# A chunk-selected attention with a mixture of experts: every expert on every token, against every expert on its own tokens

## The chip, the cores and the metric

One core of a Trainium2 chip runs the whole kernel. The time is that of one launch on the device, in microseconds (us). The engines are PE (TensorE: matmuls and transposes), ACT (ScalarE), DVE (VectorE), POOL (GpSimd) and SP (SyncE, which here only issues DMAs). A queue written SPq or PEq is the sequencer of that engine.

## The reference, cut to what matters

```python
# attention: B=4 batches, H=8 heads, S=768 positions, D=64
ub = np.sum(np.maximum(q[:, :, :, None, :] * k_min[:, :, None, :, :], q[:, :, :, None, :] * k_max[:, :, None, :, :]), axis=-1)
...
top_chunks = np.argsort(ub, axis=-1)[..., -top_k:]      # 6 of 24 chunks of 32 keys
scores = np.where(mask, scale * (q @ k.T), -1e9)         # mask: chosen chunks, causal
attn = softmax(scores); attn_out = attn @ v
x = attn_out.transpose(0, 2, 1, 3).reshape(3072, 512)

# experts: N=3072 tokens, D=512, E=8, F=512
y_dense = np.maximum(x @ w1_dense, 0.0) @ w2_dense
logits = x @ w_gate; expert_idx = np.argmax(logits, axis=1); gate_w = softmax(logits)[expert_idx]
for e in range(E):
    mask = expert_idx == e
    h = np.maximum(x[mask] @ w1[e], 0.0)
    y_moe[mask] = gate_w[mask, None] * (h @ w2[e])
out = y_dense + y_moe
```

Each token has one expert; the dense layer takes every token.

## The kernel before, in words

Tile, the framework that the kernel is written in, places the semaphores, rotates the buffers of each pool and orders the instructions of each engine by a priority that follows the order of the program, so that neighbouring steps are interleaved.

**Attention** runs over 16 pairs of heads (`p`; four to a batch). SP loads q, k and v of a pair (`load`, six DMAs of 192 KB with rows of 64 floats) two pairs ahead; POOL casts them to half precision (`cast`); PE transposes k and q (`prep_k`, `prep_q`); PE and DVE find the sixth-best chunk bound (`prep_ub`); PE transposes q with the chosen-chunk mask beside it (`prep_s`). `scores` then makes the scores of both heads for one of six pieces (PE), their exponentials (ACT, 128x1024 at a time, line 191) and the causal corners (POOL, line 195). `av` multiplies by v (line 215), and `norm` writes the result to `xbig`, which stays in SBUF. The preparation of pair p+1 is put between the pieces of pair p.

**Weights.** After attention, SP loads every weight as float32 through three staging buffers (72 pieces of 256 KB) and DVE casts each to half precision (`load_cast`, lines 276 to 278). The staging pool is closed before the pools of the next stage open on the same bytes.

**Experts.** Six groups of 512 tokens follow. For each group, 16 transposes and copies make `xT` (lines 305 and 306), the gate gives `gvec`, a weight for each token and expert that is zero except at the token's own expert (lines 312 to 327), and `layer` is called nine times: for the dense weights and for each of the eight experts, on all 512 tokens. A layer is 16 matmuls for the hidden part (line 336), four relus (line 340), 16 matmuls for the output (line 344), four copies scaled by `gvec` (line 352) and four additions to `acc` (line 353). SP stores the four `acc` tiles at the end of a group.

Of the kernel before, what the change touches and what calls it, by code (L numbers as in the profile page):

```python
# [17 lines left out]
def kernel(  # L18
# [12 lines left out]
    nc = tc.nc  # L31
# [9 lines left out]
    const = ctx.enter_context(tc.tile_pool(name="const", bufs=1))  # L41
    HP = H // 2
    NP = B * HP

# [4 lines left out]
    exf = const.tile([128, S], HF)  # L49
    nc.gpsimd.memset(exf[0:32], -30000.0)  # L50
    nc.gpsimd.affine_select(out=exf[0:32], in_=exf[0:32], compare_op=ALU.is_ge, fill=0.0,
                            base=0, pattern=[[1, S]], channel_multiplier=-32)
    nc.gpsimd.affine_select(out=exf[0:32], in_=exf[0:32], compare_op=ALU.is_ge, fill=0.0,
# [14 lines left out]
    xbig = const.tile([128, NM, Dm], HF)  # L68

    NB = 2  # L70
    kT = [[const.tile([128, S], HF, name=f"kT{i}_{g}") for g in range(2)] for i in range(NB)]
    q16 = [const.tile([128, NT, 256], HF, name=f"q16_{i}") for i in range(NB)]
    v16 = [const.tile([128, 2, NT, D + 1], HF, name=f"v16_{i}") for i in range(3)]
    for i in range(NB):
        nc.vector.memset(kT[i][0], 0.0)
        nc.vector.memset(kT[i][1], 0.0)
        nc.vector.tensor_copy(kT[i][0][0:32, :], exf[0:32])
        nc.vector.tensor_copy(kT[i][1][64:96, :], exf[0:32])
        nc.gpsimd.memset(q16[i], 0.0)
    for i in range(3):  # L80
        nc.gpsimd.memset(v16[i][:, :, :, D : D + 1], 1.0)

# [7 lines left out]
        [(5, 640, 768)],  # L90
    ]
    last_of = {}
    for pi, pc in enumerate(PIECES):
        for bb, a, z in pc:
            for t in range(a // 128, z // 128):
                last_of[t] = (pi, bb)

    with (
        tc.tile_pool(name="aload", bufs=3) as aload,
        tc.tile_pool(name="ahead", bufs=2) as ahead,  # L100
        tc.tile_pool(name="aexp", bufs=3) as aexp,
        tc.tile_pool(name="psc", bufs=2, space=bass.MemoryType.PSUM) as psc,
        tc.tile_pool(name="pout", bufs=1, space=bass.MemoryType.PSUM) as pout,
        tc.tile_pool(name="pprep", bufs=2, space=bass.MemoryType.PSUM) as pprep,
    ):
# [10 lines left out]
        def cast(p):  # L116
            s = st[p]
            s["k16"] = k16 = ahead.tile([128, NT, 2, D], HF, name="k16")
            nc.gpsimd.tensor_copy(k16, s["k"].rearrange("p g t d -> p t g d"))
            nc.gpsimd.tensor_copy(q16[p % NB][:, :, 64:192].rearrange("p t (g d) -> p t g d", g=2),  # L120
                                  s["q"].rearrange("p g t d -> p t g d"))
            nc.gpsimd.tensor_copy(v16[p % 3][:, :, :, 0:D], s["v"])
# [26 lines left out]
        def prep_ub(p):  # L149
# [13 lines left out]
            sc = q16[p % NB][:, 1:NT, :]  # L163
            sc = bass.AP(sc.tensor, sc.offset, [sc.ap[0], sc.ap[1], [192, 2], [1, NC]]) if False else None
# [4 lines left out]
        def prep_s(p):  # L169
            s = st[p]  # L170
            s["r"] = []
            for g in range(2):
                ps = pprep.tile([128, S], HF, name="pp")
                for t in range(NT):
                    nc.tensor.transpose(ps[:, t * 128 : (t + 1) * 128], q16[p % NB][:, t, g * 128 : (g + 1) * 128], ident)  # L175
                r = ahead.tile([128, S], HF, name=f"r{g}")
                nc.vector.tensor_copy(r, ps)  # L177
                s["r"].append(r)

        def scores(p, i):  # L180
            s = st[p]
            sp = psc.tile([128, 2, 512], FP, name="sp")
            wid = sum(z - a for _, a, z in PIECES[i])
            for g in range(2):
                o = 0
                for bb, a, z in PIECES[i]:
                    nc.tensor.matmul(sp[:, g, o : o + z - a], kT[p % NB][g][:, bb * 128 : (bb + 1) * 128],  # L187
                                     s["r"][g][:, a:z], start=(o == 0), stop=True, skip_group_check=True)
                    o += z - a
            ex = aexp.tile([128, 2, 512], HF, name="ex")  # L190
            nc.scalar.activation(ex[:, :, :wid], sp[:, :, :wid], AF.Exp, scale=0.125)  # L191
            o = 0
            for bb, a, z in PIECES[i]:
                if a == bb * 128:
                    nc.gpsimd.affine_select(out=ex[:, :, o : o + 128], in_=ex[:, :, o : o + 128], compare_op=ALU.is_ge,  # L195
                                            fill=0.0, base=0, pattern=[[0, 2], [1, 128]], channel_multiplier=-1)
                o += z - a
            s["ex", i] = ex

        def av(p, i):  # L200
            s = st[p]
            if i == 0:
                s["op"] = pout.tile([128, 2, 512], FP, name="op")
            op = s["op"]
            ex = s["ex", i]
            for g in range(2):
                o = 0
                seq = []
                for bb, a, z in PIECES[i]:
                    for t in range(a // 128, z // 128):  # L210
                        seq.append((t == bb, bb, t, o + t * 128 - a))
                    o += z - a
                seq.sort(key=lambda e: e[0])
                for n, (_, bb, t, c) in enumerate(seq):
                    nc.tensor.matmul(op[:, g, t * (D + 1) : (t + 1) * (D + 1)], ex[:, g, c : c + 128],  # L215
                                     v16[p % 3][:, g, bb, :], start=(i == 0 and n == 0),
                                     stop=(last_of[t] == (i, bb)), skip_group_check=True)
# [9 lines left out]

        load(0)
        load(1)
        cast(0)  # L230
        prep_k(0)
        prep_q(0)
        prep_ub(0)
        prep_s(0)
        for p in range(NP):
            if p + 2 < NP:
                load(p + 2)
            nx = p + 1 if p + 1 < NP else None
            if nx is not None:
                cast(nx)  # L240
            scores(p, 0)
            scores(p, 1)
            if nx is not None:
                prep_k(nx)
                prep_q(nx)
            av(p, 0)
            scores(p, 2)
            av(p, 1)
            if nx is not None:
                prep_ub(nx)  # L250
            scores(p, 3)
            av(p, 2)
            scores(p, 4)
            av(p, 3)
            if nx is not None:
                prep_s(nx)
            scores(p, 5)
            av(p, 4)
            av(p, 5)
            norm(p)  # L260

    WD = HF
    wpool = ctx.enter_context(tc.tile_pool(name="wpool", bufs=1))
    w1d = wpool.tile([128, NK, F], WD)
    w2d = wpool.tile([128, NK, Dm], WD)
    w1e = wpool.tile([128, NK, E, F], WD)
    w2e = wpool.tile([128, NK, E, Dm], WD)
    wg = wpool.tile([128, NK, E], WD)

    with tc.tile_pool(name="stg", bufs=3) as stg:  # L270
        wgs = stg.tile([128, NK, E], FP)
        nc.sync.dma_start(out=wgs, in_=moe_w_gate.rearrange("(ko ki) e -> ki ko e", ki=128))
        nc.vector.tensor_copy(wg, wgs)

        def load_cast(dst, src_ap):
            s2 = stg.tile(list(dst.shape), FP, tag="lc")
            nc.sync.dma_start(out=s2, in_=src_ap)
            nc.vector.tensor_copy(dst, s2)  # L278

        for ko in range(NK):  # L280
            load_cast(w1d[:, ko], moe_w1_dense[ko * 128 : (ko + 1) * 128, :])
            load_cast(w2d[:, ko], moe_w2_dense[ko * 128 : (ko + 1) * 128, :])
            for e in range(E):
                load_cast(w1e[:, ko, e], moe_w1[e, ko * 128 : (ko + 1) * 128, :])
                load_cast(w2e[:, ko, e], moe_w2[e, ko * 128 : (ko + 1) * 128, :])

    MB = 4
    with (
        tc.tile_pool(name="mx", bufs=2) as mx,
        tc.tile_pool(name="mh", bufs=3) as mh,  # L290
        tc.tile_pool(name="mts", bufs=3) as mts,
        tc.tile_pool(name="macc", bufs=2) as macc,
        tc.tile_pool(name="mg", bufs=2) as mg,
        tc.tile_pool(name="mpt", bufs=2, space=bass.MemoryType.PSUM) as mpt,
        tc.tile_pool(name="mph", bufs=2, space=bass.MemoryType.PSUM) as mph,
        tc.tile_pool(name="mpy", bufs=3, space=bass.MemoryType.PSUM) as mpy,
        tc.tile_pool(name="mpg", bufs=1, space=bass.MemoryType.PSUM) as mpg,
    ):
        for mb in range(NM // MB):
            xT = mx.tile([128, NK, MB * 128], WD)  # L300
            for mi in range(MB):
                xm = xbig[:, mb * MB + mi, :]
                for ko in range(NK):
                    tp = mpt.tile([128, 128], WD)
                    nc.tensor.transpose(tp, xm[:, ko * 128 : (ko + 1) * 128], ident)  # L305
                    nc.scalar.mul(xT[:, ko, mi * 128 : (mi + 1) * 128], tp, 1.0)  # L306

            gl = mpg.tile([128, MB, E], FP)
            gvec = mg.tile([128, MB, E], FP)
            for mi in range(MB):  # L310
# [80 lines left out]
```

## Time and profile before

| | |
|---|---|
| median of 2 runs | 662.7 us (662.58 to 662.82) |
| the profiled execution | 664.45 us, its span 662.7 us |
| mean granted TensorE clock | 0.914 of full speed |
| busy share of the span | PE 78%, ACT 59%, DVE 45%, POOL 13% |
| packets of under 512 B | 77328 of 89660 |
| HBM read, written | 37.77 MB, 6.29 MB |

The span runs from the first to the last instruction of the profiled execution. A busy share is an average over three stages with different limits, so the stages are read apart below. A granted clock of 1.0 is 2.4 GHz and one of 0.5 is 1.2 GHz.

### The profile page before, as it was taken

Reading aid. Unit: us, or ns where it says so; the run is one execution under the profiler, and the core shown is the slowest. Engines: PE = TensorE matmul, PEld = TensorE weight load, DVE = VectorE, ACT = ScalarE, POOL = GpSimd, SP = SyncE. Lnnn points to the kernel's source line nnn. Section 1 sums busy time; section 2 is a strip of 40 time slices with the busy share of each in tenths; the row PEclk is TensorE's granted clock in tenths of the full one; section 3 lists DMA queues with packets and bytes.
Section 4 is the critical chain, followed back from the end, with each engine's and each line's share of the span. In section 5 each row is a group of like instructions: output and inputs, shape, how many; then the busy total and the mean of one; then the engine's idle time right before and its main releaser. Section 6 shows DMA issues by size and latency. Waiting matters only on the chain.

```text
span 662.7 us, 9164 instructions
## 1 busy us (share of the span) xinstructions
PE 517.6 (78%) x3408; PEld 253.0 (38%) x3408; DVE 301.5 (45%) x745; ACT 393.7 (59%) x689; POOL 84.6 (13%) x164
## 2 busy tenths in 40 slices
PE   1877777775000009999899989998999899989997
PEld 1554545453000004444444444444444444444443
DVE  6777787874333331433334333343233414342343
ACT  1565666665000016777777777776777777777775
POOL 8454455532000000000000000000000000000000
PEclk9999999999555557999899989998999899999999
DMA  9996676100777750000100010001000100010001
GB/s 195 215 213 120 142 143 134 37 1 3 238 223 232 216 182 0 1 0 1 64 0 1 0 64 1 0 1 63 1 1 0 64 0 1 1 63 1 0 1 63
DMA packets 89660, 44.64 MB, mean 67 GB/s; under 512 B 77328, under 2 KB 77328, under 8 KB 89616
## 3 DMA queue, kind: packets, MB, share of 16 engines
q1 hardware_dynamic: 89616, 44.07, 27.2%
q8 instruction: 26, 0.43, 0.3%
q14 instruction: 18, 0.15, 0.1%
HBM read 37.77 MB, written 6.29 MB: 66 GB/s over the span
## 4 chain that ended last, share of the span: by engine, by line
PE 68%; DMA 11%; ACT 10%; DVE 4%; issue 4%; POOL 1%; SPq 0%; ACTq 0%; DVEq 0%; POOLq 0%
PE hp L336 30%; PE yp L344 28%; DMA s<-in_moe_w_dram 11%; ACT ex L191 8%; PE sp L187 3%; PE op L215 3%; PE tp L305 2%; ACT xT L306 1%; DVE r L177 1%; POOL ex L195 1%; PE pp L175 1%; DVE w2e L278 1%; DVE w1e L278 1%; DMA vf<-in_v_dram 1%; ACT ts L352 1%
## 5 line engine op out<-in xcount | busy, mean ns | idle before, releaser
L353 DVE TENSOR_TENSOR acc<-acc,ts 128x512 f32<-128x512 f32 x192 | 130.8, 693 | 233.6 <-ACT ts L352 233.6
L336 PE MATMUL hp<-xT,w1e 128*128 128x512 f16 x768 | 173.6, 379 | 0.0
L344 PE MATMUL yp<-w2e,hT 128*128 128x512 f16 x768 | 173.6, 379 | 0.0
L340 ACT ACTIVATE hT<-hp 128x512 f16<-128x512 f32 x216 | 129.0, 597 | 58.1 <-PE hp L336 58.1
L352 ACT ACTIVATE ts<-yp,gvec 128x512 f32<-128x512 f32 x192 | 130.0, 687 | 40.1 <-PE yp L344 40.1
L344 PEld LDWEIGHTS <-hT 128*128 128x128 f16 x864 | 80.2, 98 | 106.3 <-ACT hT L340 17.1
L191 ACT ACTIVATE ex<-sp 128x1024 f16<-128x1024 f32 x96 | 83.1, 923 | 57.2 <-PE sp L187 57.2
L336 PEld LDWEIGHTS <-w1e 128*128 128x128 f16 x768 | 75.2, 98 | 90.6
L305 PE MATMUL tp<-ident,xbig 128*128 128x128 f16 x96 | 19.3, 231 | 93.8 <-ACT xT L306 93.7
L306 ACT ACTIVATE xT<-tp 128x128 f16<-128x128 f16 x96 | 22.2, 275 | 93.1 <-DVE w2e L278 84.6
L215 PE MATMUL op<-v,ex 128*128 128x65 f16 x672 | 51.4, 196 | 27.9 <-ACT ex L191 23.7
L187 PE MATMUL sp<-r,kT 128*128 128x512 f16 (+3 forms) x256 | 62.0, 313 | 4.5 <-DVE r L177 4.5
L215 PEld LDWEIGHTS <-ex 128*128 128x128 f16 x672 | 31.6, 98 | 56.5 <-ACT ex L191 35.0
L195 POOL TENSOR_SCALAR_AFFINE_SELECT ex<-ex 128x256 f16<-128x256 f16 x96 | 38.2, 406 | 59.2 <-ACT ex L191 59.2
L305 PEld LDWEIGHTS <-xbig 128*128 128x128 f16 x96 | 9.2, 99 | 92.1 <-issue 89.6
L336 PE MATMUL hp<-xT,w1d 128*128 128x512 f16 x96 | 33.2, 495 | 0.0
L278 DVE CAST w2e<-s 128x512 f16<-128x512 f32 x32 | 13.7, 427 | 26.1 <-DMA s<-in_moe_w_dram 26.1
L278 DVE CAST w1e<-s 128x512 f16<-128x512 f32 x32 | 13.7, 427 | 21.8 <-DMA s<-in_moe_w_dram 21.8
L187 PEld LDWEIGHTS <-kT 128*128 128x128 f16 x256 | 20.9, 99 | 6.9 <-issue 6.4
L177 DVE COPY r<-pp 128x768 f16<-128x768 f16 x32 | 16.5, 553 | 11.6 <-PE pp L175 11.2
L344 PE MATMUL yp<-w2d,hT 128*128 128x512 f16 x96 | 21.7, 379 | 0.0
L162 DVE MAX8 m<-pp 128x8 f32<-128x24 f32 x160 | 16.0, 175 | 10.1 <-PE pp L156 10.1
(60 smaller groups left out, 330.3 us busy)
## 6 DMA issues: line engine op xcount, KB each, us to landing
s<-in_moe_w_dram SPq DMA_DIRECT2D x64, 256.0 KB, 3.0
kf<-in_k_dram SPq DMA_DIRECT2D x32, 192.0 KB, 4.3
qf<-in_q_dram SPq DMA_DIRECT2D x32, 192.0 KB, 3.6
vf<-in_v_dram SPq DMA_DIRECT2D x32, 192.0 KB, 4.3
out_dram<-acc SPq DMA_DIRECT2D x24, 256.0 KB, 2.1
s<-in_moe_w_dense_dram SPq DMA_DIRECT2D x8, 256.0 KB, 3.1
wgs<-in_moe_w_gate_dram SPq DMA_DIRECT2D x1, 16.0 KB, 4.5
```

The source lines that it names most:

```text
L187: nc.tensor.matmul(sp[:, g, o : o + z - a], kT[p % NB][g][:, bb * 128 : (bb + 1) * 128], s["r"][g][:, a:z], start=(o == 0), stop=True, ski ...
L191: nc.scalar.activation(ex[:, :, :wid], sp[:, :, :wid], AF.Exp, scale=0.125)
L195: nc.gpsimd.affine_select(out=ex[:, :, o : o + 128], in_=ex[:, :, o : o + 128], compare_op=ALU.is_ge, fill=0.0, base=0, pattern=[[0, 2], [ ...
L215: nc.tensor.matmul(op[:, g, t * (D + 1) : (t + 1) * (D + 1)], ex[:, g, c : c + 128], v16[p % 3][:, g, bb, :], start=(i == 0 and n == 0), s ...
L278: nc.vector.tensor_copy(dst, s2)
L305: nc.tensor.transpose(tp, xm[:, ko * 128 : (ko + 1) * 128], ident)
L306: nc.scalar.mul(xT[:, ko, mi * 128 : (mi + 1) * 128], tp, 1.0)
L336: nc.tensor.matmul(hp, w1ap[:, ko, j * 128 : (j + 1) * 128], xT[:, ko, :], start=(ko == 0), stop=(ko == NK - 1),)
L340: nc.scalar.activation(hT[:, j, :], hp, AF.Relu)
L344: nc.tensor.matmul(yp, hT[:, j, mi * 128 : (mi + 1) * 128], w2ap[:, j, :], start=(j == 0), stop=(j == NK - 1),)
L352: nc.scalar.activation(ts, yp, AF.Copy, scale=gvec[:, mi, e : e + 1])
L353: nc.vector.tensor_add(accs[mi], accs[mi], ts)
```

## The change

**Sort.** `out` is computed from each token's own expert only. Half-precision `xbig` rows get 16 more elements, the first two of which hold the gate weight; each batch of 768 tokens is written to a DRAM tile `xd`, and its dense result, in float32, to a DRAM tile `yd`. After the last batch a counting sort on chip (two matmuls for ranks and totals, a chain of DVE operations, 24 one-hot matmuls) assigns the tokens to 31 blocks of 128 rows, each block of one expert; 31 is enough for any distribution (24 full blocks and up to seven that padding opens). All 31 always run.

**Blocks.** For each block POOL issues a gather of 128 rows of `xd` (1056 bytes each), a gather of 128 rows of `yd` (2 KB each) and a scatter of 128 rows to `out` (2 KB each; padding rows are skipped by a bound). PE does 4 transposes, 4 matmuls of 512 columns, 4 transposes and 4 matmuls, with the weights addressed by an offset in a PE register. One DVE operation scales by the gate weight and adds the dense row.

**Dense layer and gate** of a batch become 21 short steps (`fills`), one of which is put after every second unit of the next batch's attention; those of the last batch run after attention.

**Weights** are loaded by POOL-issued DMAs that cast on the way, straight into place: the dense ones at the start, one half of an expert with each pair.

**Attention** works in 11 units of one head (exponentials of 128x512) where it had six pieces of both, with scores two units ahead, loads three pairs ahead and three buffers where there were two; a third set of `kT` and `q16` is initialised.

```diff
+    def load_dense():
+        nc.gpsimd.dma_start(out=wg, in_=moe_w_gate.rearrange("(ko ki) e -> ki ko e", ki=128))
+        nc.gpsimd.dma_start(out=wd[:, 0:NK], in_=moe_w1_dense.rearrange("(ko ki) f -> ki ko f", ki=128))
+        nc.gpsimd.dma_start(out=wd[:, NK:], in_=moe_w2_dense.rearrange("(ko ki) f -> ki ko f", ki=128))
+    def load_expert(e, w):
+        src = moe_w1 if w == 0 else moe_w2
+        nc.gpsimd.dma_start(out=we[:, e, w * NK : (w + 1) * NK], in_=src[e].rearrange("(ko ki) f -> ki ko f", ki=128))
...
+    def batch_fills(b):
...
+                for ko in range(NK):
+                    nc.tensor.transpose(tp[:, ko], xbig[:, b * NT + mi, ko * 128 : (ko + 1) * 128], ident)
+                nc.vector.tensor_copy(xT[:, :, mi * 128 : (mi + 1) * 128], tp)
...
+            nc.sync.dma_start(out=xd[b * S : (b + 1) * S].rearrange("(m p) w -> p m w", p=128),
+                              in_=xbig[:, b * NT : (b + 1) * NT].bitcast(U16))
...
+                    nc.tensor.matmul(hp, wd[:, ko, j * 128 : (j + 1) * 128], xT[:, ko, g * G * 128 : (g + 1) * G * 128],
+                                     start=(ko == 0), stop=(ko == NK - 1))
+                nc.scalar.activation(hold["h"][:, j], hp, AF.Relu)
...
+                    nc.tensor.matmul(yp, hold["h"][:, j, i * 128 : (i + 1) * 128], wd[:, NK + j],
+                                     start=(j == 0), stop=(j == NK - 1))
+                ys = my.tile([128, Dm], FP, name="ys")
+                evac(ys, yp)
+                m = b * NT + g * G + i
+                nc.sync.dma_start(out=yd[m * 128 : (m + 1) * 128], in_=ys)
...
+        seq = [(p, u) for p in range(NP) for u in range(NU)]
...
+            if u == 0:
+                if p + 3 < NP:
+                    load(p + 3)
+                if wq:
+                    load_expert(*wq.pop(0))
...
+            if fills and u % 2 == 1:
+                fills.pop(0)()
+            av(p, u)
...
+        for m in range(NM):
+            nc.vector.tensor_scalar(Am[:, m, :], io128, rf[:, m : m + 1], None, ALU.is_equal)
+            nc.tensor.matmul(pm, Am[:, m, :], Bm[:, m], start=(m == 0), stop=(m == NM - 1))
+            if m % 3 == 0 and d:
+                d.pop(0)()
...
+        _, offs = nc.values_load_multi_w_load_instructions(
+            eo[:, 0:NBLK], engines=[mybir.EngineType.PE], min_val=0, max_val=(E - 1) * 2 * NK * 512,
...
+        def gather(i):
+            s = es[i]
+            s["x"] = xg = eg.tile([128, XW], U16, name="xg")
+            nc.gpsimd.indirect_dma_start(out=xg, out_offset=None, in_=xd,
+                                         in_offset=bass.IndirectOffsetOnAxis(ap=gi[:, i : i + 1], axis=0))
+            s["y"] = yg = eg.tile([128, Dm], FP, name="yg")
+            nc.gpsimd.indirect_dma_start(out=yg, out_offset=None, in_=yd,
+                                         in_offset=bass.IndirectOffsetOnAxis(ap=gi[:, i : i + 1], axis=0))
...
+        def e1(i):
+            s = es[i]
+            hp = p2.tile([128, 512], FP, name="hp", tag="h")
+            for ko in range(NK):
+                nc.tensor.matmul(hp, s["xT"][:, ko], wef[:, bass.ds(offs[i] + ko * 512, 512)],
+                                 start=(ko == 0), stop=(ko == NK - 1))
+            s["h"] = h = et.tile([128, 512], HF, name="eh")
+            nc.scalar.activation(h, hp, AF.Relu)
...
+        def e2(i):
...
+            o = eg.tile([128, Dm], FP, name="yo")
+            nc.vector.scalar_tensor_tensor(o, yp, s["x"][:, Dm : Dm + 2].bitcast(FP), s["y"], ALU.mult, ALU.add)
+            nc.gpsimd.indirect_dma_start(out=out, out_offset=bass.IndirectOffsetOnAxis(ap=si[:, i : i + 1], axis=0),
+                                         in_=o, in_offset=None, bounds_check=N - 1, oob_is_err=False)
...
+        for i in range(NBLK):
+            e1(i)
+            if i + 2 < NBLK:
+                gather(i + 2)
+            if i + 1 < NBLK:
+                tx(i + 1)
+            if i > 0:
+                e2(i - 1)
+            th(i)
+        e2(NBLK - 1)
```

`tx` transposes the four quarters of a gathered block and copies them on DVE; `th` does the same for the hidden part, with the copy on ACT. The pool `eg` holds three buffers of each gathered tile and of `yo`.

## Rows read from the trace of the kernel before

**Rows 1.** The page's 40 slices of the span, busy tenths and granted clock.

```profile
PE   1877777775000009999899989998999899989997
PEclk9999999999555557999899989998999899999999
DMA  9996676100777750000100010001000100010001
```

**Rows 2.** Busy time of each engine by stage; last columns: granted clock, DMA share, GB/s.

```profile
0.00:18.00 18.00, 4.00 (x35) 2.90 (x36) 10.96 (x27) 2.09 (x2) 14.08 (x27) 1.00 1.16 197
18.00:162.50 144.50, 111.88 (x1456) 70.82 (x1455) 108.77 (x332) 91.87 (x111) 70.55 (x137) 0.99 0.58 113
162.50:250.00 87.50, 2.68 (x20) 1.57 (x20) 33.04 (x83) 2.86 (x14) 0.00 (x0) 0.51 0.68 207
388.00:457.00 69.00, 67.02 (x322) 30.07 (x322) 25.12 (x54) 50.14 (x98) 0.00 (x0) 0.98 0.04 16
```

**Rows 3.** Chain that ended last, pieces in order of time: start, length, what.

```profile
320.82 1.69 PE hp L336 x4
...
329.04 3.45 PE hp L336 x16
...
389.85 1.71 PE hp L336 x4
```

**Rows 4.** Groups of instructions by line and form: count, busy us, mean ns.

```profile
L336 PE MATMUL hp<-xT,w1e 128*128 128x512 f16 x768 | 173.6, 379 | 0.0
L344 PE MATMUL yp<-w2e,hT 128*128 128x512 f16 x768 | 173.6, 379 | 0.0
L353 DVE TENSOR_TENSOR acc<-acc,ts 128x512 f32<-128x512 f32 x192 | 130.8, 693 | 233.6 <-ACT ts L352 233.6
L340 ACT ACTIVATE hT<-hp 128x512 f16<-128x512 f32 x216 | 129.0, 597 | 58.1 <-PE hp L336 58.1
L191 ACT ACTIVATE ex<-sp 128x1024 f16<-128x1024 f32 x80 | 78.7, 1032 | 57.2 <-PE sp L187 57.2
L177 DVE COPY r<-pp 128x768 f16<-128x768 f16 x32 | 16.5, 553 | 11.6 <-PE pp L175 11.2
L119 POOL CAST k<-kf 128x768 f16<-128x768 f32 x16 | 13.2, 825 | 6.5 <-PE pp L128 5.2 <-DMA kf<-in_k_dram 1.0
L321 DVE TENSOR_SCALAR onehot<-gl,mxv 128x8 f32<-128x8 f32 x24 | 5.2, 217 | 0.0
L79 POOL MEMSET q<- 128x1536 f16 x2 | 2.9, 1470 | 0.1
```

**Rows 5.** Busy time by stage: attention's start and middle, the weight loads.

```profile
32.00:50.00 18.00, 13.84 (x187) 8.97 (x186) 14.57 (x45) 11.55 (x15) 9.89 (x19) 1.00 1.14 216
104.00:122.00 18.00, 13.85 (x188) 8.93 (x186) 14.38 (x45) 11.55 (x15) 9.52 (x18) 1.00 0.64 139
164.00:246.00 82.00, 0.00 (x0) 0.00 (x0) 30.31 (x72) 0.00 (x0) 0.00 (x0) 0.50 0.73 221
```

**Rows 6.** DMA issues: count, KB each, median us from issue to landing.

```profile
s<-in_moe_w_dram SPq DMA_DIRECT2D x64, 256.0 KB, 3.0
kf<-in_k_dram SPq DMA_DIRECT2D x32, 192.0 KB, 4.3
out_dram<-acc SPq DMA_DIRECT2D x24, 256.0 KB, 2.1
```

**Rows 7.** Timeline: start, length, engine, line, operation, count.

```profile
10.16 1.72 SPq L114 DMA_DIRECT2D kf<-in_k_dram  x2
...
90.76 0.78 PE L175 MATMUL pp<-ident,q 128*128 128x128 f16 x11
...
318.69 0.24 PE L312 MATMUL gl<-wg,xT 128*128 128x8 f16 x4
```

**Rows 8.** Busy time in short stretches: where the clock falls; columns as Rows 2.

```profile
60.00:64.00 4.00, 2.76 (x51) 2.13 (x50) 1.74 (x14) 1.76 (x3) 1.19 (x4) 1.00 0.65 116
64.00:68.00 4.00, 3.72 (x26) 2.31 (x23) 3.19 (x6) 2.03 (x3) 2.80 (x5) 0.59 0.47 106
```

More of the change, by code (lines that the diff above doesn't have):

```diff
@@ new lines @@
+    ohp = const.tile([128, E, NM + 1], HF)
+    nc.gpsimd.memset(ohp, 0.0)
+    segm = const.tile([128, E, NM + 1], FP)
+    nc.gpsimd.memset(segm, 1.0)
+    nc.gpsimd.memset(segm[:, :, 0:1], 0.0)
+    ones = const.tile([128, 128], HF)
+    nc.gpsimd.memset(ones, 1.0)
+    low = const.tile([128, 128], HF)
+    nc.gpsimd.memset(low, 1.0)
+    nc.gpsimd.affine_select(out=low, in_=low, compare_op=ALU.is_gt, fill=0.0,
+                            base=0, pattern=[[1, 128]], channel_multiplier=-1)
+    io128 = const.tile([128, 128], HF)
@@ L167, in prep_ub, with prep_s @@
                                         m8[:, 1:NT, g, 5:6].to_broadcast([128, NT - 1, NC]), ALU.is_lt)
-        def prep_s(p):
+        def prep_s(p, g):
             s = st[p]
[L171 to L178, printed above, removed]
@@ L180, in scores @@
-        def scores(p, i):
-            s = st[p]
[L182 to L191, printed above, removed]
-            o = 0
-            for bb, a, z in PIECES[i]:
+            ps = pprep.tile([128, S], HF, name="pp")
@@ L226, in norm @@
                 opv[:, :, :, 0:D], rs.to_broadcast([128, 2, NT, D]), ALU.mult)
+        for kind in ("tr", "h", "y"):
+            cur[kind] = (pfill, "fb")
         load(0)
         load(1)
+        load(2)
+        load_dense()
         cast(0)
+        cast(1)
         prep_k(0)
@@ L233 @@
         prep_ub(0)
[L234 to L285, printed above, removed]
@@ new lines @@
+        prep_k(1)
+        prep_q(1)
+        prep_s(0, 0)
+        prep_s(0, 1)
+        wq = [(e, w) for e in range(E) for w in range(2)]
+        ahead_n = 2
+        seq = [(p, u) for p in range(NP) for u in range(NU)]
+        for i in range(ahead_n):
+            scores(*seq[i])
+        for i, (p, u) in enumerate(seq):
+            n1 = p + 1 if p + 1 < NP else None
+            n2 = p + 2 if p + 2 < NP else None
+            if u == 0:
+                if p + 3 < NP:
+                    load(p + 3)
+                if wq:
+                    load_expert(*wq.pop(0))
+                if n2 is not None:
+                    cast(n2)
+            if i + ahead_n < len(seq):
+                scores(*seq[i + ahead_n])
+            if u == 0 and n1 is not None:
+                prep_ub(n1)
+            if u == 4 and n1 is not None:
+                prep_s(n1, 0)
+            if u == 5 and n1 is not None:
+                prep_s(n1, 1)
+            if u == 7 and n2 is not None:
+                prep_k(n2)
+            if u == 8 and n2 is not None:
+                prep_q(n2)
+            if fills and u % 2 == 1:
+                fills.pop(0)()
+            av(p, u)
+            if u == NU - 1:
+                norm(p)
+                if p % HP == HP - 1 and p + 1 < NP:
+                    a, d = batch_fills(p // HP)
+                    fills += a + d
```

352 lines of the change are left out of this document (247 added, 105 removed).

## The prediction

> **What bounds the kernel now.** I read the slices first [rows 1], then the engines by stage [rows 2]. The reader is to see three stages with three limits. In attention (18 to 162.5 us, 16 pairs, 9.0 us each) PE is busy 77%, DVE 75%, ACT 64%: no engine is full, and hand-overs between engines set the pace. In the weight stage (162.5 to 250) PE does almost nothing while DMAs bring 18.9 MB. In the expert stage (250 to 662.7) PE is busy 67.0 of every 69.0 us. The chain [rows 3] names the same thing: a group of 512 tokens every 69.0 us (320.82 to 389.85), and a run of 16 matmuls of 512 columns in 3.45 us, so 0.216 us each. The means of 379 ns [rows 4] contain overlap and are not used as costs of a matmul in a stream. The profiled execution took 664.45 us, 1.75 more than its span; the median of the runs shown is 662.7, the same as the span, so my sum of spans is compared with the median directly.
>
> **The experts' matmuls.** Before, 2 x 768 matmuls [rows 4] x 0.216 = 332 us serve the experts. After, 31 blocks x 8 = 248 x 0.216 = 54 us: this is the gain to be had, plus the weight stage's 82 us of idle PE [rows 5], plus gaps in attention. What replaces it has four parts.
>
> **Start, 18 to 27 us.** POOL opens with constants and only then casts. It gets a third memset of 1.47 us [rows 4], some ten small constants (at a fifth of that, 3 us) and three dense loads to issue. The trace has no DMA issued by POOL. SP's issue takes 0.86 us where its queue is full [rows 7]; a landing takes 2.1 us at the shortest and 4.3 at the longest [rows 6]. An issue of POOL lies above SP's, since POOL must itself make 128 rows or more, and below a landing if it doesn't wait for one. I take 1.5, the middle of 0.86 and 2.1; for the range, 0.9 and 3. So 1.5 + 3 + 4.5 = 9 us later; 4 if the scheduler puts the loads behind the casts.
>
> **Attention with dense steps, 165 us.** By engine, per pair, from [rows 5] (18 us hold two pairs): PE 6.9, DVE 7.2, ACT 5.8, POOL 4.8. Halving the exponentials costs ACT five more fixed parts: 2 x 597 - 1032 = 162 ns each [rows 4], 0.8 us. The dense steps of a batch cost PE 24 transposes at 0.071 and 24 gate matmuls at 0.06 [rows 7], 32 matmuls of 384 columns at 0.162 and 24 of 512 at 0.216: 13.5 us, 3.4 for each of four pairs. DVE gets six copies of 512 (two thirds of 0.553 us [rows 4]), about eight gate operations at 0.22 and three evacuations at 0.69: 1.5 per pair. ACT gets eight relus, three copies: 1.5 per pair. So PE 10.3, DVE 8.7, ACT 8.1 in the twelve later pairs, and PE becomes the bound. Before, the period was 1.25 times the busiest engine; finer units, three score banks and scores two units ahead remove most of the waits, and I take 11.0 (10.3 if all go). The first four pairs have no dense step: between 7.2 and 9.0, I take 8.3. 4 x 8.3 + 12 x 11.0 = 165.
>
> DMA is the cover here. The 18.9 MB of q, k and v move at 216 GB/s with the DMA share at 1.1 [rows 5], 88 us. The 18.9 MB of weights moved at 221 GB/s with a share of 0.73, so about 300 GB/s when full: 62 us. Three quarters of the writes of `xd` and `yd`, 7.1 MB, add 24. Together 174 of 192 us. It fits, barely; if it doesn't, loads come late (a rival below). SP's queue holds the loads three pairs ahead and now the stores of `xd` and `yd` before them, each waiting for its step: a load stands behind a store, which three buffers cover. On POOL an expert load (1.5 us) and a cast wait ahead of the corners, with 4.8 + 1.5 + 1 of 11 us in use. For the casting loads I keep 62 us; if a load that casts goes half as fast, 124.
>
> **Between attention and the first block, 24 us.** The norm, six transposes with copies (2.4), the gate (1.7), then the sort: some 30 DVE operations of 0.2 to 0.9 us on small tiles (0.217 for the smallest [rows 4]), 24 comparisons of 128 columns at 0.22, four evacuations: about 20 us of DVE in a chain, and some ten hand-overs. The last batch's dense steps on PE (10 us) lie beside it. PE's loading of 31 registers shows in no row: nothing if hidden behind DVE, 7 us if it stands on the chain and each costs what the smallest DVE operation does; I take nothing, and 7 for the upper end.
>
> **The 31 blocks, 155 us.** Per block, PE needs 8 x 0.216 + 8 x 0.071 = 2.3 us at full clock; at half clock a matmul takes 0.42 (1.69 for four [rows 3]), so 4.5. ACT: 0.6 + 0.45. DVE: 0.37 + 0.69 [rows 4]. DMA engines: 0.66 MB at 300 GB/s, 2.2. POOL issues three: 4.5. Buffers: a gather waits until block i-3 has used its data; one block's way (issue 1.5, landing 3, two transposes with copies 1.6, two rounds of matmuls with relu 2.8, addition 0.7, hand-overs 1.2) is 10.8, over three buffers 3.6. POOL is the longest, half-clock PE close behind; with 0.5 us for waits on its queue I take 5.0: a scatter stands on POOL's queue for its addition with the next gathers behind it. 31 x 5.0 = 155, and 10 us to fill and drain (the first landing and chain, the last scatter's landing).
>
> Sum: 27 + 165 + 24 + 155 + 10 = 381, so 380 us. Low: 22 + 4 x 7.2 + 12 x 10.3 + 18 + 31 x 4.0 + 8 = 325. High: 27 + 173 + 31 + 31 x 6.6 + 14 = 450.
>
> **The rivals.** *Landings in a row.* If POOL's queue waits for each transfer to land, a block takes 3.0 + 3.0 + 2.1 = 8.1 us [rows 6] and the whole 226 + 251 = 477. Against it: SP issued two 192 KB loads in 1.72 us [rows 7] that landed in 4.3 each, so landings overlap there. The Trainium skill (DMA: Bandwidth & Descriptors, "Anatomy of one DMA — SWDGE (gpsimd) path") gives such a DMA a fixed 2.0 us or so, mostly completion, plus bytes over 436 GB/s. By that 256 KB lands in 2.6 us, between this trace's 2.1 and 3.0, and a block of this rival (2.3 + 2.6 + 2.6) would end the kernel at 226 + 31 x 7.5 = 458. Chance 0.08.
>
> *The clock stays low.* In attention PE was busy 2.76 of 4 us and the clock fell to 0.59 in the next 4 [rows 8]; the blocks would leave PE less busy. With 4.5 us of PE at half clock, in order, and two hand-overs a block that it can't fill, 6.5 us: 226 + 202 = 428. Against it: at that pace PE is busy again, as in the expert stage at 0.98 [rows 2]. Chance 0.15.
>
> *Attention starves.* If casting loads take 124 us of DMA time instead of 62, the DMA sum is 235 and attention ends some 45 us later: 425. For it: a DMA share above 1 in the first 50 us already [rows 5]. Chance 0.08.
>
> *POOL and DVE shut each other out.* If POOL can issue only while DVE rests, a block takes 4.5 + 1.1 + 0.5 = 6.1 and the whole 415. Against it: POOL's 16 casts average 825 ns [rows 4] beside a DVE busy three quarters of the time. The Trainium skill (SBUF — State Buffer, "SBUF: two separate sides") warns that a POOL-issued DMA can't write its descriptors while DVE runs certain two-port operations, mostly SBUF to SBUF. The two large DVE operations of a block read PSUM, so it should seldom apply; no row here shows it. Chance 0.04.
>
> *Slower than before.* If each block's gathers waited for the scatter before them (through the buffers or an order kept on `out`), a block would be serial: two issues 3.0, landing 4.3, the chain at half clock 8.1, issue 1.5, landing 4.3: 21 us, 226 + 657 = 883. It decides from (662.7 - 226) / 31 = 14.1 us per block. Against it: three buffers, and gathers read tiles that no scatter writes. Chance 0.02. That the work isn't cut can't be: the loop over 31 blocks is written out.
>
> **How the numbers follow.** My forecast, 325 to 420, has 0.62; the rivals 0.08, 0.15, 0.08, 0.04 and 0.02; 0.01 is left for no difference. A measurement of this kernel tells about 2% from no change. All but the last two cases are faster by far more: 0.97, 0.01, 0.02. The range, 325 to 450, leaves out the landings in a row, the serial case and the tails of the sums.
>
> **What would show it.** The period of a pair: 8.3, then 11 us with PE the fullest. The first gather near 216. A block every 5 us with POOL's three issues at 1.5 us as the fullest row, and the waits of PE's transposes on gathers. If POOL's issues take under 1 us, PE's hand-overs set the pace and the blocks end sooner; if over 2, the blocks alone pass 200 us. A granted clock near 0.5 in the last stage speaks for the second rival, waits of casts on q, k and v for the third. The prediction is wrong mostly if the price of a POOL issue is, since each 0.1 us of it moves the end by 9 us.

## The result, and the profile after

The changed kernel takes **394.3 us** (median; 394.07 to 394.51), 0.595 of the time before (95% interval 0.5924 to 0.5975). The prediction was 380, with a range of 325 to 450. The profiled execution took 394.51 us, its span 392.8.

| part | predicted | profiled |
|---|---|---|
| start to first scores | 27 | 28.2 |
| attention | 165 | 185.2 (28.2 to 213.4, the end of the last norm) |
| to the first gather | 24 | 21.7 (to 235.1) |
| 31 blocks | 155 (5.0 each) | 143.6 (31 x 4.63; gathers at 235.1 to 374.1, 30 periods) |
| fill and drain | 10 | 14.1 |
| sum | 381 | 392.8 |

So the sum comes within 12 us by luck in part, because two errors cancel: attention is 20 us longer than predicted, the blocks 11 shorter. The mean of 4.63 us per block holds a start-up: the first three gathers are issued at once, the fourth 13.2 us after the third (251.0), and from the fourth on they come every 4.56 us. The slices of the page, to be held against [rows 1]:

```profile
PE   0157377157599989999898872667555658565660
PEclk9998869779699999999999996888989996989895
DMA  9999999999997886211031425143444444444440
```

The weight stage, in which PE did nothing, is gone. PE is at 9 only in the second half of attention. In the first 11 slices (108 us) the DMA row stands at 9 and PE at 7 at most: that is the first thing to explain. In the last 15 slices no row shown is full: the second thing.

**Attention.** Busy time by stage (columns as in [rows 2]) shows its two halves:

```profile
60.00:80.00 20.00, 8.20 (x112) 5.12 (x112) 10.17 (x38) 6.33 (x13) 7.12 (x17) 0.85 1.08 187
120.00:140.00 20.00, 19.43 (x229) 12.76 (x228) 15.98 (x49) 15.27 (x30) 10.83 (x28) 1.00 0.85 203
```

From 120 to 140 us PE is busy 19.4 of 20 us (19.3 from 160 to 180), and the norms of `xbig` come every 10.0 us (105.8 to 175.8, seven periods; predicted 11.0, PE the fullest: right). From 60 to 80 PE is busy 8.2 of 20, with a DMA share of 1.08. The DMA view of 14 to 70 us says what moved (issues, KB each, median us from issue to landing):

```profile
q0 software_dynamic: 7198, 6.64, 73.3%
q1 hardware_dynamic: 19786, 4.96, 50.8%
...
we<-in_moe_w_dram POOLq DMA_DIRECT2D x12, 512.0 KB
...
kf<-in_k_dram SPq DMA_DIRECT2D x8, 192.0 KB, 9.1
qf<-in_q_dram SPq DMA_DIRECT2D x8, 192.0 KB, 9.4
```

Twelve of the sixteen expert loads are issued by 70 us, where the program's place for the twelfth is the twelfth pair, and k and q take 9.1 and 9.4 us to land, where in the kernel before, from 14 to 60 us with the DMA row as full and no software queue, they took 4.5 and 3.9. Who waits stands in the waits of 27 to 120 us (us in total, times, longest), of PE and then of POOL:

```profile
PE op L362 <- POOL ex L344: 29.7, 8, 9.4
```

```profile
POOL q L269 <- DMA qf<-in_q_dram: 20.9, 4, 7.6
POOL ex L344 <- ACT ex L334: 11.4, 21, 3.0
POOL k L268 <- DMA kf<-in_k_dram: 8.1, 2, 5.3
```

Casts of q and k stand on POOL for their data, the causal corners (`ex`, line 344) stand behind them on the same queue, and PE waits 29.7 us for corners.

**Blocks.** Groups by line and form, as in [rows 4]:

```profile
L523 POOL DMA_INDIRECT xg<-xd,gi x31 | 30.3, 977 | 41.5 <-DVE yo L561 21.6
L526 POOL DMA_INDIRECT yg<-yd,gi x31 | 29.4, 949 | 10.5 <-issue 10.2
L562 POOL DMA_INDIRECT out_dram<-yo,si x31 | 31.5, 1015 | 15.3 <-issue 13.4
L561 DVE SCALAR_TENSOR_TENSOR yo<-yp,xg,yg 128x512 f32<-128x512 f32 x31 | 23.3, 750 | 31.9 <-PE yp L558 27.2
```

Each of POOL's operations takes 0.95 to 1.02 us, with some 0.30 behind it: 1.28, where 1.5 was taken. Three are 3.85 of a block's 4.63 us. The rest is the gather's wait for the addition (L561), and it does not come in every block. The timeline of two blocks (start, length, engine, line, operation):

```profile
297.20 0.97 POOL L523 DMA_INDIRECT xg<-xd,gi  x1 [1.89 <-DMA out_dram<-yo,si]
298.48 0.95 POOL L526 DMA_INDIRECT yg<-yd,gi  x1 [0.30 <-issue]
299.73 1.02 POOL L562 DMA_INDIRECT out_dram<-yo,si  x1 [0.30 <-issue]
...
301.06 0.98 POOL L523 DMA_INDIRECT xg<-xd,gi  x1 [0.31 <-DVE exT L535]
...
304.62 0.40 PE L533 MATMUL tp<-ident,xg 128*128 128x128 f16 x4 [2.08 <-DMA xg<-xd,gi]
304.86 0.59 PE L558 MATMUL yp<-we,ehT 128*128 x2
...
305.49 0.75 DVE L561 SCALAR_TENSOR_TENSOR yo<-yp,xg,yg 128x512 f32<-128x512 f32 x1
...
306.51 0.98 POOL L523 DMA_INDIRECT xg<-xd,gi  x1 [1.89 <-DVE yo L561]
```

Read from 297.20: POOL's three operations, 3.86 us, until the next gather at 301.06; that gather's issue and landing, 3.56, until PE can transpose its rows at 304.62; then the last two of the four output matmuls of the block before, which PE's order puts behind these transposes, the addition, and the release, 1.89, until the next gather at 306.51. That is 9.31 us for two blocks, a loop in which one landing stands whole. The gather waits because with three buffers it takes the ones that this addition frees.

The granted clock was 1.00 in this loop, so no slow clock made it long. Of the 13 such loops from 251.03 to 370.24, the six with a granted clock of 1.00 take 8.5 to 10.0 us (mean 8.9), the seven with 0.71 to 0.91 take 8.8 to 10.1 (mean 9.4). By these means the lower clock costs some 4 us over the 31 blocks, an estimate.

The drain, on the same timeline:

```profile
383.51 0.98 POOL L562 DMA_INDIRECT out_dram<-yo,si  x1 [1.86 <-DMA out_dram<-yo,si]
386.37 0.98 POOL L562 DMA_INDIRECT out_dram<-yo,si  x1 [1.88 <-issue]
```

With nothing between them, the last three scatters stand 2.85 us apart (the first of them at 380.66). The row at 383.51 names the wait: the landing of the scatter before it; both write `out`. In the loop this is hidden.

### The profile page after: what moved, and what is told of

Its sections match the earlier page's. It is cut to its first block, busy times and chain, and to the rows that moved or that the text cites. A ratio compares the mean times of both kernels' runs of the same rounds, so it can differ in the third digit from the quotient of the medians.

```text
span 392.8 us, 7052 instructions
## 1 busy us (share of the span) xinstructions
PE 258.8 (66%) x2426; PEld 152.8 (39%) x2426; DVE 192.1 (49%) x538; ACT 159.7 (41%) x303; POOL 208.0 (53%) x370
## 5 line engine op out<-in xcount | busy, mean ns | idle before, releaser
L334 ACT ACTIVATE ex<-sp 128x512 f16<-128x512 f32 (+1 forms) x176 | 91.7, 585 | 63.1 <-PE sp L330 31.1
L344 POOL TENSOR_SCALAR_AFFINE_SELECT ex<-ex 128x128 f16<-128x128 f16 (+1 forms) x176 | 52.2, 306 | 55.9 <-ACT ex L334 53.0
L362 PE MATMUL op<-v,ex 128*128 128x65 f16 x672 | 47.6, 200 | 34.6 <-POOL ex L344 29.7
L535 DVE COPY exT<-tp 128x512 f16<-128x512 f16 x31 | 13.2, 425 | 80.5 <-PE tp L533 59.3
L523 POOL DMA_INDIRECT xg<-xd,gi x31 | 30.3, 977 | 41.5 <-DVE yo L561 21.6
L541 PE MATMUL hp<-we,exT 128*128 x124 | 37.4, 432 | 10.2 <-DVE exT L535 5.8
L558 PE MATMUL yp<-we,ehT 128*128 x124 | 38.8, 419 | 4.5 <-ACT ehT L552 2.6
L562 POOL DMA_INDIRECT out_dram<-yo,si x31 | 31.5, 1015 | 15.3 <-issue 13.4
L561 DVE SCALAR_TENSOR_TENSOR yo<-yp,xg,yg 128x512 f32<-128x512 f32 x31 | 23.3, 750 | 31.9 <-PE yp L558 27.2
L526 POOL DMA_INDIRECT yg<-yd,gi x31 | 29.4, 949 | 10.5 <-issue 10.2
L217 PE MATMUL hp<-xT,wd 128*128 128x384 f16 x128 | 26.5, 325 | 0.7 <-ACT hT L219 0.3
L226 PE MATMUL yp<-wd,hT 128*128 128x512 f16 x96 | 24.6, 378 | 1.5 <-DVE xbig L371 1.0
```

The source lines that it names most:

```text
L217: nc.tensor.matmul(hp, wd[:, ko, j * 128 : (j + 1) * 128], xT[:, ko, g * G * 128 : (g + 1) * G * 128], start=(ko == 0), stop=(ko == NK - 1))
L226: nc.tensor.matmul(yp, hold["h"][:, j, i * 128 : (i + 1) * 128], wd[:, NK + j], start=(j == 0), stop=(j == NK - 1))
L334: nc.scalar.activation(ex[:, :o], sp[:, :o], AF.Exp, scale=0.125)
L344: nc.gpsimd.affine_select(out=exd, in_=exd, compare_op=ALU.is_ge, fill=0.0, base=0, pattern=[[0, n], [1, 128]], channel_multiplier=-1)
L523: nc.gpsimd.indirect_dma_start(out=xg, out_offset=None, in_=xd, in_offset=bass.IndirectOffsetOnAxis(ap=gi[:, i : i + 1], axis=0))
L526: nc.gpsimd.indirect_dma_start(out=yg, out_offset=None, in_=yd, in_offset=bass.IndirectOffsetOnAxis(ap=gi[:, i : i + 1], axis=0))
```

## The experiments

**Expert loads kept where the program puts them.** The program asks for half an expert with each pair; a load waits for nothing, and the scheduler moved it ahead.

```diff
-        nc.gpsimd.dma_start(out=we[...], in_=src[e].rearrange(...))
+        tc.keep_in_program_order(
+            nc.gpsimd.dma_start(out=we[...], in_=src[e].rearrange(...)))
```

> Same kernel, but each expert load is kept behind what was written before it on POOL, so that one goes out per pair (before: all 16 issued by 89 us). Theory (the weights' early traffic makes q, k and v land late, and a cast that waits for them holds the causal corners behind it on POOL): the first seven pairs come down from some 13 us to 10 or 11, attention ends 15 to 25 us earlier, total 370 to 380, and q, k and v land in 4 to 5 us throughout. Rival (DMA is simply full in attention, it is the amount of bytes that counts): the same wait only moves to later pairs, total within 5 us of 394.

Measured: 366.4 us, 0.553 of before (0.5521 to 0.5539). The issues of the loads (ns min/median/max, first and last start), of the changed kernel and then of this one:

```profile
L126 POOL DMA_DIRECT2D we<-in_moe_w_dram x16: 742/757/760, 20.2 to 88.9; - x16
```

```profile
L127 POOL DMA_DIRECT2D we<-in_moe_w_dram x16: 757/757/764, 30.6 to 178.8; - x16
```

And the stretch 60 to 80 us of this kernel, by stage as above:

```profile
60.00:80.00 20.00, 15.21 (x228) 10.76 (x225) 16.57 (x56) 12.81 (x25) 12.31 (x30) 1.00 1.02 183
```

PE is busy 15.2 us where it was 8.2, at much the same DMA share. Attention ends at 187.4 instead of 213.4: 26 of the gain of 28 us are there, and blocks stay at 4.61 us. The same bytes cost 26 us less when the loads are spread.

The gain is larger than the theory's range, and one part of the expectation failed: k and q still take 8.4 and 7.4 us to land from 14 to 70 us, not 4 to 5. What changed is how much of them gets through a DMA row that is full in both kernels. The queues of that stretch in this kernel (q1 carries q, k and v, q0 the casting loads), to be held against 4.96 and 6.64 MB above:

```profile
q1 hardware_dynamic: 30043, 7.54, 73.4%
q0 software_dynamic: 3875, 3.34, 42.3%
```

**No expert loads but the first.**

```diff
-    wq = [(e, w) for e in range(E) for w in range(2)]
+    wq = [(0, w) for w in range(2)]
...
-        nc.vector.tensor_scalar(eo[:, 0:NBLK], ef, float(E - 1), float(2 * NK * 512), ALU.min, ALU.mult)
+        nc.vector.tensor_scalar(eo[:, 0:NBLK], ef, float(E - 1), 0.0, ALU.min, ALU.mult)
```

> Leaves out the loads of experts 1 to 7, and every block uses expert 0's weights. Measures what the 14.7 MB of loads left out cost in attention. If they are what slows the first seven pairs: attention ends near 185 to 190 us in place of 213, total 366 to 372. If pairs stay at 12 to 15 us there, the new order of units and casts on POOL is to blame, total 390 or more.

Measured: 371.0 us (one run), attention's end at 187.5. Leaving out 14.7 MB of casting loads gains nothing over spreading them: attention has room for their DMA time; what cost it 26 us was their place.

**Dense steps after attention** (with the loads spread): the lines that put a step after every second unit are left out, so all steps run when attention is done.

```diff
-            if fills and u % 2 == 1:
-                fills.pop(0)()
```

> Weights one load per pair, and no dense step between attention's units: the dense layers of the first three batches run after attention, ahead of the last one's. Theory of the prediction (the dense steps make PE the bound of the later pairs, some 2 us a pair, and run hidden otherwise): pairs fall from 10 to 8 us, attention ends near 165 in place of 187, and the dense steps then take 36 to 42 us by themselves; total 378 to 390. Rival (they cost the pairs nothing): attention still ends near 185, total 400 or more.

Measured: 387.5 us (one run). Without steps the pairs are a steady 8.64 us apart and attention ends at 166.5, 21 us earlier; the first gather is at 226.0 instead of 209.1, 17 later. In 120 to 140 us:

```profile
120.00:140.00 20.00, 15.93 (x220) 11.02 (x220) 15.95 (x57) 14.47 (x28) 13.09 (x33) 0.93 0.83 139
```

PE has room for the steps, though not for free: the interleaving is worth 21 us (387.5 - 366.4), 17 of them before the first gather.

**Five buffers** in `eg`, on the changed kernel:

```diff
-        tc.tile_pool(name="eg", bufs=3) as eg,
+        tc.tile_pool(name="eg", bufs=5) as eg,
```

> Five buffers in place of three for the gathered tiles and the result of a block. Theory (in the blocks POOL's queue would do a block in 3.85 us, three times 0.98 busy and 0.3 between; the 4.63 us measured contain waits for a free buffer in every second block): a block takes 3.9 us, total 370 to 374. Rival (landing of the gather and PE's chain set the pace, not the number of buffers): a block stays at 4.5 us or more, total 390 or more.

Measured: 381.7 us, 0.5757 (0.5738 to 0.5775), between the theory's total and its rival's. Gathers come every 3.68 us (234.5 to 344.8), as fast as POOL issues with its scatters lagging, but the scatters fall behind: the last is at 373.6, 28.8 us after the last gather; the theory's total had left that out. DVE now waits for scatters to land (240 to 380 us):

```profile
DVE yo L561 <- DMA out_dram<-yo,si: 43.6, 20, 5.8
```

So the buffers held the gathers back, and the order of the scatters is the next bound.

**One gather per block**, on the changed kernel, with three buffers: x and y of a token lie in one row of 3104 bytes of one DRAM tile.

```diff
-    xd = dram.tile([N, XW], U16, name="xd")
-    yd = dram.tile([N, Dm], FP, name="yd")
+    xd = dram.tile([N, XW + 2 * Dm], U16, name="xd")
...
-            s["y"] = yg = eg.tile([128, Dm], FP, name="yg")
-            nc.gpsimd.indirect_dma_start(out=yg, out_offset=None, in_=yd, ...)
+            s["y"] = xg[:, XW:].bitcast(FP)
```

> The dense rows are stored beside the rows of x in one DRAM tile, so that a block needs one gather of 3104-byte rows in place of two; three buffers as before. Theory (POOL's issues are what a block is made of): POOL needs 2 x 1.28 = 2.6 us, and the three buffers then bind at about 3.6, total 360 to 368. Rival (bytes or landings bind, the issues don't): at least 4.5 us a block, total 388 to 396, or more since rows of 2 KB are now stored with gaps.

Measured: 399.3 us, 0.6043 (0.6007 to 0.6079), 4.66 us per block: a third less work on POOL gains nothing, and the theory fell. A loop of two blocks in this kernel's timeline, at a granted clock of 1.00:

```profile
310.14 0.97 POOL L523 DMA_INDIRECT xg<-xd,gi  x1 [3.56 <-DVE yo L559]
...
312.74 0.97 POOL L523 DMA_INDIRECT xg<-xd,gi  x1 [0.30 <-issue]
...
316.77 0.40 PE L531 MATMUL tp<-ident,xg 128*128 128x128 f16 x4 [0.37 <-DMA xg<-xd,gi]
...
318.66 0.97 POOL L523 DMA_INDIRECT xg<-xd,gi  x1 [2.61 <-DVE yo L559]
```

POOL's part is 2.60 us, from gather to transposes it is 4.03, the rest 1.89: 8.52. The changed kernel's loop at 306.51, also at 1.00, has 3.87, 2.80 and 1.88: 8.55. What POOL gave up, the landing took back: the transposes need x alone and now wait for the bytes of y as well. (A landing has a median of 4.0 us here; for x alone it is 2.9 in the five-buffer run.) So the run doesn't show that POOL's operations cost nothing, since they stand in the loop; it shows that the time doesn't follow them alone.

The clock hides part of it. The loop before this one and this one, by engine (columns as in [rows 2]):

```profile
300.69:310.14 9.45, 6.27 (x33) 3.02 (x31) 2.35 (x4) 2.32 (x4) 3.99 (x5) 0.82 0.44 140
310.14:318.66 8.52, 5.17 (x35) 2.54 (x34) 2.35 (x4) 2.41 (x5) 3.98 (x4) 1.00 0.50 155
```

Of the 13 loops from 254.05 to 375.90 only four have a granted clock of 1.00, and they take 8.3 to 8.6 us; the nine at 0.70 to 0.83 take 9.1 to 11.2. At 1.00 the one gather would gain some 0.2 us per block on the changed kernel's mean, an estimate from these loops.

**The output matmuls ahead of the next block's transposes**, on the changed kernel:

```diff
             e1(i)
+            if i > 0:
+                e2(i - 1)
             if i + 2 < NBLK:
                 gather(i + 2)
             if i + 1 < NBLK:
                 tx(i + 1)
-            if i > 0:
-                e2(i - 1)
             th(i)
```

> Only the order of the block loop changes: the second product of block i-1 is written before the gather of block i+2 and the transposes of block i+1. In the changed kernel's list for PE those transposes stand in the middle of that product (two matmuls, four transposes, two matmuls), in every second block. Theory (a product that stands behind the next gather's landing frees its buffer late, and the gather after that waits for the buffer: a loop of waits, three buffers or not): a block falls from 4.63 to 3.9 to 4.2 us, total 372 to 382. Rival (POOL's queue and the landings set 4.6 whatever PE's order is): 390 or more.

Measured: 403.5 us, 0.6078 (0.6054 to 0.6102), 4.97 us per block; the theory that the place of these matmuls alone costs the time fell. In program order the scatter now also stands ahead of the next gather, and POOL waits in front of it:

```profile
302.16 0.98 POOL L523 DMA_INDIRECT xg<-xd,gi  x1 [0.30 <-PE hp L541]
...
307.68 1.86 PE L558 MATMUL yp<-we,ehT 128*128 x4
...
310.61 1.02 POOL L562 DMA_INDIRECT out_dram<-yo,si  x1 [2.35 <-DVE yo L561]
...
311.94 0.98 POOL L523 DMA_INDIRECT xg<-xd,gi  x1 [0.30 <-PE hp L541]
```

In the 9.78 us lie one landing, PE's hidden and output matmuls one after the other (1.87 and 1.86 us), an addition and a scatter. One wait took the place of another. How much the new order loses is not shown, since the clock has a part in it: of eleven loops of two blocks the three at a granted clock of 1.00 take 8.1 to 8.9 us, the eight at 0.82 to 0.84, the one shown among them, take 9.3 to 10.4.

**Which buffers, and does the scatter's place on POOL's queue matter?** Two kernels on the version with its loads spread (366.4 us, three buffers). The first gives `yo` alone five buffers:

```diff
+        tc.tile_pool(name="ego", bufs=5) as ego,
...
-            o = eg.tile([128, Dm], FP, name="yo")
+            o = ego.tile([128, Dm], FP, name="yo")
```

> On the version with its expert loads spread (366.4 us): five buffers instead of three for the sums yo alone, the gathered tiles stay at three. Theory (a gather waits for the addition three blocks back, which frees xg and yg; that addition stands on PE behind the transposes of the next gathered block): nothing changes, 4.6 us per block, 363 to 369 us. Rival (the release of yo, which waits for a scatter to land, is what the five buffers of the earlier run bought): 3.7 to 4.0 us per block at the gathers, under 358 us.

Measured: 365.0 us, 0.5514 (0.5502 to 0.5526), 4.63 us per block: nothing. The second leaves the scatter out:

```diff
-            nc.gpsimd.indirect_dma_start(out=out, out_offset=..., in_=o, ...)
+            nc.sync.dma_start(out=out[i * 128 : (i + 1) * 128] if i < NM else pad[...], in_=o)
```

> On the version with its expert loads spread (366.4 us), three buffers: the scatter is left out; SP stores yo in the order of the blocks, the first 24 to out and seven to a scratch tile, so POOL issues two gathers per block and no DMA waits for one before it (out holds the rows in the order of the blocks). Theory (the release of xg and yg by the addition sets the pace): 4.2 to 4.6 us per block, 350 to 364 us. Rival (POOL's queue, on which the scatter stands between the gathers, sets it): 2.6 us of POOL per block, at most 3.4 us per block, under 335 us.

Measured: 354.1 us, 4.36 us per block (208.5 to 339.2). Even without a scatter on POOL or any order on `out`, gathers wait for the addition (240 to 345 us):

```profile
POOL xg L525 <- DVE yo L563: 46.2, 13, 4.6
```

Both say the same: the release of `xg` and `yg` by the addition sets the pace with three buffers. In the loop from 276.74 to 285.54 POOL's part fell from 3.86 to 2.52 us, and the time from gather to transposes grew by 0.83 over that of the changed kernel's loop shown above.

**The edits together**: loads spread, one gather, five buffers; then with the order of matmuls of above as well.

> Weights one load per pair, one gather per block, five buffers, all together. Theory (one gather alone brought nothing because the wait for buffers bound; with both mended POOL needs 2.6 us a block, and each scatter waits some 1.9 us for the one before it to land, so 2.9 at least): a block takes 3.0 to 3.3 us, total 318 to 330. Rival (PE, at a clock below full, or the bytes bind next): 3.7 us or more, total 340 or more.

Measured: **341.4 us, 0.515 of before (0.5125 to 0.5175)**, the shortest time of a kernel that does the whole computation. Gathers come every 3.21 us, scatters every 3.60 (227.9 to 336.0); this is neither the theory's 318 to 330 nor much more than its rival's bound. At the end a scatter waits for the one before it to land:

```profile
330.34 0.98 POOL L561 DMA_INDIRECT out_dram<-yo,si  x1 [2.47 <-DMA out_dram<-yo,si]
```

> The same with the second product first in the loop. If five buffers already break the loop of waits: within 4 us of the run without it. If PE's order still costs: 5 to 15 us less.

Measured: 345.6 us, 0.5218 (0.5205 to 0.5231): with five buffers the order of PE's matmuls buys nothing, and costs some 4 us, just over the 4 of the expectation.

**What is the one gather worth there, and what the scatters' order?** The first kernel is the same with two gathers (the edits of the first and the fourth experiment); the second is the version at 341.4 us with its scatter replaced as above.

> Loads spread and five buffers, but x and y gathered apart as in the changed kernel: it separates the two edits in the version at 341.4 us. Theory (with five buffers POOL's three issues bind, 3 x 1.28 = 3.85 us per block, plus the scatters' waits): 350 to 357 us. Rival (the landing of the scatter before it sets each scatter, so a gather more on POOL is hidden in that wait): 339 to 345 us.

Measured: 354.2 us, 0.5373 (0.5339 to 0.5407). Scatters come every 4.04 us (221.9 to 343.1). One gather, worth nothing at three buffers, is worth 12 to 13 us at five.

> The version at 341.4 us (loads spread, one gather per block, five buffers) with the scatter left out in the same way: plain stores by SP in the order of the blocks, seven blocks to a scratch tile (out holds the rows in the order of the blocks). Theory (there each scatter waits for the landing of the scatter before it, 3.6 us per block): without it the end follows the gathers, 3.0 to 3.2 us per block or less, 312 to 326 us. Rival (something else sets the pace, PE and the additions): still 3.5 us or more per block, 335 us or more.

Measured: 307.9 us (two runs, 305.2 and 310.6, the first of them profiled), below the expected 312 to 326. Gathers come every 2.63 us (209.6 to 288.3), and now PE is full (240 to 300 us):

```profile
240.00:300.00 60.00, 53.14 (x368) 26.92 (x366) 27.65 (x47) 27.72 (x47) 19.05 (x20) 1.00 0.78 246
```

So at 341.4 us the scatter costs some 36 us, by the faster run: its 1.3 us on POOL per block, and the landing that each one waits for. How much of the two each has was not told apart, and whether scatters that don't wait for each other could be had with the same output was not tried.

## Why the prediction held, and where its steps did not

*The gain.* The 332 us of experts' matmuls became 31 blocks, and PE's idle weight stage went under attention: as predicted, and far larger than all errors below. No rival came in as a whole.

*Attention, 165 us: 185.* The step that failed is the cover: "Together 174 of 192 us. It fits, barely". The sum was sound (with the loads spread, attention takes some 160 us and ends at 187.4); what failed is the assumption that half an expert is loaded with each pair. With twelve loads out by 70 us, q, k and v got 4.96 MB through from 14 to 70 us, where with the loads spread they get 7.54. The starvation rival named the symptom, waits of casts on q and k, and put it down to casting loads that move at half speed. That cause is refuted: all of the 26 us come back with the same loads at other times, and none more when 14.7 MB of them are left out. With the loads spread a pair from the fourth on takes 9.9 us (67.5 to 186.4, twelve periods; 11.0 predicted). The first three periods, with no dense steps, are 9.4 us on average (39.2 to 67.5) and not 8.3; with all steps moved out, pairs settle at 8.64. So 8.3 was short by one and 11.0 long by one; with the loads spread the two cancel in part, and attention is 6 us shorter than predicted.

*Start and the sort, 27 and 24: 28.2 and 21.7.* The sums are right, the start's by luck. POOL's first cast comes 6.3 us later (15.56, before 9.27) and not 9: POOL's issue of an expert load takes 0.757 us, half of the 1.5 taken, and even lies below SP's 0.86 [rows 7]. The other 3.8 us the prediction did not have: the preparation of the second pair now stands ahead of the first scores on PE and DVE (21.9 to 27.3).

*A POOL issue at 1.5: 1.28.* By the prediction's own rule ("each 0.1 us of it moves the end by 9 us") this should have given 20 us, a block of 4.3. The block took 4.63. The step that failed is "POOL is the longest". Its row is no fuller than PE's (busy 34.5 against 38.0 of 60 us from 240 to 300, 39.0 against 38.3 from 300 to 360), and its three operations are one of three terms: taking a third of them away gained nothing, and two more buffers bought 12.6 us. The buffers' loop was costed as one block's way, 10.8 us over three buffers, 3.6 per block. That division supposes that three blocks are always on their way at once. The loop of the trace is another: gather i+2 waits for the addition of block i-1, which waits for two matmuls, which stand on PE behind the transposes of block i+1, which wait for gather i+1 to land. Two blocks cost POOL's operations, one landing and the tail in a row: 3.86 + 3.56 + 1.89. With five buffers this loop is gone and "three issues" is the right answer for the gathers: 3.68. The upper end of the range did not use the 3 us that the prediction had named for an issue: three of those are 9 us a block, and the sum has 6.6.

*Waits on POOL's queue.* The prediction's "a scatter stands on POOL's queue for its addition" costs little in the changed kernel, where the gathers' wait comes first and the scatter finds its sum ready; it is what e2_first ran into (40.6 us over the 31 blocks).

*The rivals.* Landings in a row: refuted as stated, though half true, since one landing of two stands in the loop. The Trainium skill (DMA: Bandwidth & Descriptors, "Anatomy of one DMA — SWDGE (gpsimd) path") gives a fixed 2.0 us plus bytes over 436 GB/s, by which 256 KB takes an estimated 2.6 us; in the five-buffer run the y gathers of that size have a median of 3.3 from issue to landing, and the measurement decides. The clock: the granted clock is 0.62 in the first 12 us of gathers (235 to 247), 0.85 from 240 to 300 and 0.91 from 300 to 360, not near 0.5; by the loops above it costs some 4 us. POOL and DVE: the y gather at 298.48 takes 0.95 us beside the addition of 298.25 to 299.00, and all 31 of them take 0.945 to 0.960, so no exclusion shows. The serial case: the order on `out` exists, with 2.85 us between scatters, but the gathers don't wait for it; it was wrong as a price for the block and is the floor after the buffers.

*Fill and drain, 10: 14.1.* The last three scatters follow each other by their landings. The 14.1 are the drain alone; the start-up, 13.2 us between the third and the fourth gather, lies in the row of the blocks. In it the load of the 31 offsets, which the prediction took at nothing, stands on PE's queue for 2.80 us (from 240.9), and PE is idle for 3.26 before the first block's matmuls. The prediction compared its sum of spans with the median directly; every run on record takes 1.7 to 2 us more than its span, too little to matter here.

Open: why the gathers' landings grow where the scatter is left out (median for x from 2.8 to 3.2 us, 240 to 300 us, both with the loads spread), and what lowers TensorE's clock in some loops and not in others; the runs show that it happens, not why.

## What to carry to other kernels

A buffer loop is not one item's way divided by the buffers: follow who frees the buffer, what stands before that instruction in its engine's order, and whether a landing lies in between. An engine's operations are a bound only if taking some away moves the end; here taking a third of POOL's away gained nothing until two buffers more were there, and then 12 to 13 us. Before a run is read as a refutation, hold loops of the same granted clock against each other. A load that waits for nothing is issued when the scheduler likes: where the DMA engines are nearly full, fix its place, and look behind its queue for what arrives late instead.

## What was not expected of the hardware

POOL's time for an indirect DMA of 128 rows doesn't depend on the bytes of a row: 0.977 us at 1056 bytes, 0.949 at 2 KB, 0.97 at 3104, 1.015 for a scatter of 2 KB, each with 0.30 behind it. A 512 KB load that casts is issued in 0.757.

A 192 KB load of SP beside a full DMA row (shares of 0.97 to 1.24) lands the later, the more of the DMA time in these four stretches a software queue takes: 4.5 us for k and 3.9 for q with none (kernel before, 14 to 60 us), 4.6 for both at 5% (most expert loads left out, 30 to 70), 8.4 and 7.4 at 42% (loads spread, 14 to 70), 9.1 and 9.4 at 73% (changed kernel, 14 to 70).

Much the same busy time went with different clocks: 0.79 in the blocks of the one-gather kernel (240 to 300 us, PE busy 36.5 of 60, part of it at the lower clock), 1.00 with loads spread, five buffers and two gathers (38.1 of 60). Four matmuls of 512 columns take 1.02 us in some blocks and 1.86 in others of the same run.
